# An attention head's pauses filled, its queues reordered, and four weight splits moved to a late head

## The chip, the cores and the metric

The kernel runs on one core of a Trainium2 chip, as one launch. The metric is the device time of that launch in microseconds (us). TensorE (PE) multiplies matrices, its weight loads are listed apart (PEld), VectorE (DVE) and ScalarE (ACT) work on both on-chip memories, GpSimd (POOL) on SBUF alone, and SyncE (SP) issues most of the DMAs. Each engine runs its own queue in order; engines wait for one another by semaphores.

## The reference

Two batches of eight heads of attention, in which a query sees only the keys of its own hash bucket, then a layer of eight experts in which each token goes to its two best, then a second layer in which it goes to one. Only the attention is changed here:

```python
q_bits = (np.einsum('bhsd,dk->bhsk', q, proj) > 0).astype(np.int64)   # 6 bits; the same for k
mask = q_bucket[:, :, :, None] == k_bucket[:, :, None, :]
scores = np.where(mask, scale * np.matmul(q, k.transpose(0, 1, 3, 2)), -1e9)
attn = np.exp(scores - np.max(scores, axis=-1, keepdims=True))
attn = attn / (np.sum(attn, axis=-1, keepdims=True) + 1e-09)
out = np.matmul(attn, v)                       # q, k, v: (2, 8, 768, 64)
```

## The kernel before, in words

**Heads and blocks.** The 16 heads (two batches of eight) run one after another, 768 queries against 768 keys each. The keys are cut into six tiles of 128. The work is software-pipelined: while head i is computed, the maxima of head i+1 are taken, and head i+2 is loaded and prepared. The order of everything is written out by hand: `FIRST` (L1617) for head 0 and `STEPS` (L1609) for the others are six blocks of words, and `step` carries out one word after the other. A word such as `split 0 2 v p` names the step, the head relative to i, the tile, and the engines (a ScalarE, v VectorE, p GpSimd). Instructions stand in each engine's queue in that order.

**The steps of a head.** `hi` and `lo` cut the queries (`QA`, `QB`) and keys (`KA`, `KB`) into a rounded part and a rest (L216 or L218, L223). `hash` (L229) multiplies by the projection, `mask` (L235) turns the signs into rows of QA and KA. `max` (L244, L246) multiplies 128 queries with all keys on TensorE, and VectorE reduces the product to one column; `neg` and `row` (L250, L256, L260) put the six results back into QA as a row. `scores` (L275, L278) are four matmuls of 384 columns and the exponential on ScalarE (L280, tile `P`, two buffers). `split` copies P into a rounded `Ph` (L216 on ScalarE or L218 on VectorE) and subtracts it, `Pl` = P - Ph (L287, on GpSimd; tile 5, and all tiles of the last head, on VectorE). `values` (L298) are six matmuls of 386 columns with Ph and Pl. `z` (L265) is an activation on ScalarE that each head has once, near its end; `mean`, `turn` and `out` finish the head before.

**Buffers.** Every `max`, `scores`, `hash`, `row`, `mean` and `turn` takes one of three PSUM tiles named `big`. A matmul into one waits until the reader of its former content is done. The matmuls without use, `warm(n)` (L193), multiply constants of 512 columns in bf16 into the tile `pv`; before the loop over the heads they stand between the first steps.

**Weight splits.** The experts' weights arrive as halves of 512 KB (tile `wst`, four buffers; four are loaded in head 1). `Experts.split` rounds one half on ScalarE (`whi`, L486), subtracts on VectorE (`wlo`, L489), and asks SP for the next half (the fourth early split asks for none). Four splits are done early, one each in heads 4 to 7 at the word `x` in block 1. The list `early` holds such work with its place, (head, "x") or (head, block); `extra` runs it there.

**Gates of the first batch.** In heads 8 to 15 the list has the routing of the first batch: `parts` (four small VectorE steps, L562 to L565, head 13), `hot` (six comparisons against slot numbers, L644, head 14), `trim` (L616, L617: which of the first 128 places overflow, head 14 behind `hot`), `table` and `fetch` (head 14, block 2), `turn` (head 15).

Of the kernel before, what the change touches and what calls it, by code (L numbers as in the profile page):

```python
# [373 lines left out]
class Experts:  # L374
# [327 lines left out]
    def turn(self, X, xs, u, st, ps=None):  # L702
        nc = self.nc
        xh, xl = X[:, 0], X[:, 1]
        sz = u.sizes[st]
        if ps is None:
            ps = self.mp.tile([128, 4, 128], F32, name="pt", bufs=2)
        for kt in range(4):
            nc.tensor.transpose(ps[:, kt, 0:sz], xs[st][0:sz, kt * 128:(kt + 1) * 128], self.ident[0:sz, 0:sz])
        s = slice(st * 128, st * 128 + sz)  # L710
        nc.scalar.activation(xh[:, :, s], ps[:, :, 0:sz], AF.Copy)
        nc.vector.tensor_sub(xl[:, :, s], ps[:, :, 0:sz], xh[:, :, s].bitcast(F32))  # L712
# [903 lines left out]
)  # L1616
FIRST = (  # L1617
# [6 lines left out]
)  # L1624
# [2 lines left out]
def lsh_moe_kernel(tc, qk, v, proj, w_gate, w_noise, noise, w1, w2, w2_gate, w21, w22, cst_in, out):  # L1627
    nc = tc.nc
    with ExitStack() as ctx:
# [11 lines left out]
        with ExitStack() as actx:  # L1641
            xp = actx.enter_context(tc.tile_pool(name="xp", bufs=3))
            at = Attention(tc, actx, qk, v, cst)
            X = {}
            n = B * H

            def big():
                return at.pb.tile([128, 2, 512], F32, name="big")

            def done(i):  # L1650
                b, h = divmod(i, H)
                if h % 4 == 0:
                    X[b, h // 4] = xp.tile([128, NJ, DM // 2], F32, name="x")
                return at.c_out(i, X[b, h // 4], lg[:, b], i == n - 1)

            def store(b, c0, c1):
                nc.sync.dma_start(xd[b * S:(b + 1) * S, c0:c1].rearrange("(p j) d -> p j d", j=NJ), X[b, c0 // 256][:, :, c0 % 256:(c1 - 1) % 256 + 1])

            def after(i):
                b, h = divmod(i, H)  # L1660
                if h in (3, 5, 7):
                    store(b, *{3: (0, 256), 5: (256, 384), 7: (384, 512)}[h])

            at.load(0)
            at.setup(proj)
            nc.sync.dma_start(cst[:, 128:], cst_in[:, 128:C_CUT])
            nc.sync.dma_start(cst[:, 0:128], cst_in[:, 0:128])
            at.consts2()
            at.load(1)
            nc.sync.dma_start(at.mask, cst_in[96:96 + NJ, C_MASK:C_MASK + S])  # L1670
            at.gate_consts(w_gate, w_noise)
            at.load_v(0)
            at.load_v(1)
            at.load(2)
            at.load_v(2)
            at.warm(9)
            at.a_hash(0)
            at.warm(5)
            at.a_hi(0, "KA")
            at.a_hi(0, "QA", nc.vector)  # L1680
            at.a_mask(0, "KA")
            at.a_mask(0, "QA", slice(0, 1))
            at.a_mask(0, "QA", slice(1, 2))
            at.a_hi(0, "KB")
            at.a_hi(0, "QB")
            at.a_lo(0, "KB", nc.gpsimd)
            at.a_lo(0, "QB", nc.gpsimd)
            for j in range(NJ):
                at.b_max(0, j)
                at.warm((1, 1, 1, 1, 0, 0)[j])  # L1690
                if j == 1:
                    at.a_hi(1, "KA")
                    at.a_hi(1, "QA")
                if j == 4:
                    at.v_hi(0, nc.gpsimd)
                    at.v_lo(0, nc.gpsimd)
            ex = Experts(tc, cst, consts, wpool, ((w1, w2), (w21, w22)), noise, w2_gate, at, lg,
                         ld[:, :], [t[:, :] for t in td])
            ex.carry = carry
            ex.rows_in = cst_in[:, C_ROWS:C_END]  # L1700
            at.b_neg(0)
            at.a_hash(1)
            at.b_row(0, 2)
            at.a_mask(1, "QA")
            at.a_mask(1, "KA")
            at.a_hi(1, "KB")
            at.a_hi(1, "QB")
            early = []

            *_, chain = gates = ex.gate1(0)  # L1710
            scale = gates[0]
            ratio, first, parts = ex.weights1(0)
            hot, table, fetch, turn = ex.early_table(Unit(0, 128, 0, range(0, NJ)), at.wk, big, xd[0:S, :])
            for i in range(4):
                early.append(((4 + i, "x"), lambda i=i: ex.split(i % 2)))
            for (h, s), f in (
                    ((0, 4), scale), *(((1, "x"), f) for f in chain[0:2]), ((2, "x"), chain[2]),
                    *(((3, "x"), f) for f in chain[3:]), ((3, 5), lambda: ex.ranks(slice(0, NJ), big()[:, 0])),
                    ((4, "x"), ratio), ((4, "x"), first), ((5, "x"), parts),
                    ((6, "x"), lambda: hot((0, 1, 2))), ((6, "x"), lambda: hot((3, 4, 5))), ((6, "x"), ex.trim),  # L1720
                    ((6, 2), table), ((6, 2), fetch), ((7, "x"), lambda: ex.rest_ranks(big()[:, 0])),
                    ((7, 2), lambda: turn(0))):
                early.append(((H + h, s), f))

            def extra(i, s):
                for at_, f in early:
                    if at_ == (i, s):
                        f()

            def step(i, s, op):  # L1730
                o, *a = op.split()
                k = i + int(a[0])
                a = a[1:]
                if not 0 <= k < n:
                    return
                e = [dict(a=nc.scalar, v=nc.vector, p=nc.gpsimd)[x] for x in a if x in "avp"]
                if o in ("scores", "values"):
                    getattr(at, "c_" + o)(k, int(a[0]))
                elif o == "split":
                    if k == n - 1:  # L1740
                        e[1] = nc.vector
                    at.c_split(k, int(a[0]), *e)
                elif o in ("move", "mean", "turn"):
                    getattr(at, "c_" + o)(k)
                elif o == "out":
                    done(k)
                    after(k)
                elif o == "x":
                    extra(i, "x")
                elif o == "load":  # L1750
                    at.load(k)
                    at.load_v(k)
                elif o == "max":
                    at.b_max(k, int(a[0]))
                elif o in ("neg", "row"):
                    getattr(at, "b_" + o)(k)
                elif o == "hash":
                    at.a_hash(k)
                elif o == "mask":
                    at.a_mask(k, a[0])  # L1760
                elif o in ("hi", "lo"):
                    getattr(at, "a_" + o)(k, a[0], e[0])
                elif o == "z":
                    at.z_row(k)
                elif k % 2 == 0:
                    getattr(at, o)(k, e[0])

            for i in range(n):
                nx, n2 = i + 1 < n, i + 2 < n
                for s in range(NJ):  # L1770
                    for op in (FIRST if i == 0 else STEPS)[s]:
                        step(i, s, op)
                    extra(i, s)
                    if i == 1 and s == 3:
                        for _ in range(NST):
                            ex.load()
                    if i in (2, 3, 4, 5) and s == 3:
                        ex.clear(yd[:, :], i - 2)
            ps = big()[:, 0]
            u0 = Unit(0, 128, 0, range(0, NJ))  # L1780

            def rows(*r):
                ex.early_rows(u0, *r, ps)

            at.c_values(n - 1, 4)
            rows(0, 4)
            at.c_values(n - 1, 5)
            at.c_move(n - 1)
            rows(4, 9)
            at.c_mean(n - 1)  # L1790
            rows(9, 12)
            at.c_turn(n - 1)
            rest = done(n - 1)
            rest()
            after(n - 1)
# [39 lines left out]
```

## Time and profile before

| | |
|---|---|
| median of 3 runs | 855.6 us (855.22 to 859.2) |
| the profiled execution's own time | 851.21 us |
| its span, first to last instruction | 849.4 us |
| mean granted TensorE clock in it | 0.976 |
| head 0, its scores to its `z` | about 17 to 36 us |
| heads 1 to 15, `z` to `z` | 13.7 to 18.8 us each, the last `z` at 286.5 us |

The page of the profile gives each engine's busy share and a strip of 40 slices; the views used below are the instructions in order of time (the timeline), and the busy time of every engine in chosen stretches (windows). A row of windows has, in this order: the stretch, its length, the busy time and the instructions of PE, PEld, DVE, ACT and POOL, the granted share of TensorE's full clock, the DMA engines' busy share and GB/s. The stretches called heads here run from one `z` (L265) to the next: that of head i holds its blocks 0 to 3, and blocks 4 and 5 of head i-1. The attention ends at about 296 us; the two expert layers take the rest and are not changed.

### The profile page before, as it was taken

How to read it: one execution, taken by the hardware profiler on the slowest of the kernel's cores; microseconds unless marked ns; L12 is line 12 of the kernel's file. 1: busy time of each engine (PE TensorE's matmuls, PEld its weight loads, DVE VectorE, ACT ScalarE, POOL GpSimd, SP SyncE). 2: the span in 40 equal slices, each digit the busy share in tenths (PEclk: the TensorE clock that was granted, in tenths of full speed). 3: DMA queues.
4: the chain of work that ended last, by engine and by line, in shares of the span. 5: the costliest groups of instructions: out<-in, count | busy, mean ns of one | idle time of the engine just before them, and what ended most of it. 6: DMA issues, size and time to landing. Idle time of an engine off the chain costs nothing. (4 is left out here: it accounts for less than half of the span.)

```text
span 849.4 us, 14032 instructions
## 1 busy us (share of the span) xinstructions
PE 798.8 (94%) x5260; PEld 721.9 (85%) x5260; DVE 568.2 (67%) x1086; ACT 466.2 (55%) x649; POOL 378.2 (45%) x302
## 2 busy tenths in 40 slices
PE   7799999999999995899999999999999889999996
PEld 3688777878887784899999999999998789999996
DVE  7688899879897573566645453546485767875654
ACT  5688989898886641244343443334342235555653
POOL 7568776767676015551415050504121253444221
PEclk9899999999999996899999999999999999999999
DMA  5135264022011023266444453435231727787871
GB/s 138 42 116 186 69 222 118 1 75 51 7 38 32 1 69 113 63 203 205 135 167 142 135 194 108 151 124 191 94 129 61 242 83 228 247 262 244 254 247 50
DMA packets 84773, 111.17 MB, mean 131 GB/s; under 512 B 20975, under 2 KB 59007, under 8 KB 84700
## 3 DMA queue, kind: packets, MB, share of 16 engines
q1 hardware_dynamic: 75164, 86.76, 32.5%
q0 software_dynamic: 9312, 23.25, 8.0%
q8 instruction: 44, 0.72, 0.4%
q14 instruction: 29, 0.24, 0.1%
q10 hardware_dynamic: 224, 0.20, 0.1%
HBM read 90.95 MB, written 19.72 MB: 130 GB/s over the span
## 5 line engine op out<-in xcount | busy, mean ns | idle before, releaser
L489 DVE TENSOR_TENSOR wlo<-wst,whi 128x1024 fp32r<-128x1024 f32 x129 | 157.1, 1231 | 36.3 <-ACT whi L486 35.9
L287 POOL TENSOR_TENSOR Pl<-P,Ph 128x768 fp32r<-128x768 f32 x75 | 145.4, 1945 | 73.5 <-ACT Ph L216 30.3
L486 ACT ACTIVATE whi<-wst 128x1024 fp32r<-128x1024 f32 x129 | 134.1, 1053 | 11.5 <-DMA wst<-in_moe_w_dram 11.3
L737 PE MATMUL mm<-xh,whi 128*128 128x400 f32 (+7 forms) x416 | 135.0, 325 | 4.0 <-issue 2.1
L738 PE MATMUL mm<-xh,whi 128*128 128x400 f32 (+7 forms) x416 | 131.9, 317 | 1.8 <-DVE xh L712 1.0
L739 PE MATMUL mm<-xh,wlo 128*128 128x400 f32 (+7 forms) x416 | 131.6, 316 | 1.5 <-issue 1.4
L743 ACT ACTIVATE hh<-mm 128x400 fp32r<-128x400 f32 (+7 forms) x104 | 45.4, 440 | 151.9 <-PE mm L739 123.0
L737 PE MATMUL mm<-hh,whi 128*128 128x400 f32 (+5 forms) x320 | 107.8, 337 | 1.0 <-issue 1.0
L738 PE MATMUL mm<-hh,whi 128*128 128x400 f32 (+5 forms) x320 | 104.7, 327 | 0.3 <-issue 0.3
L739 PE MATMUL mm<-hh,wlo 128*128 128x400 f32 (+5 forms) x320 | 104.4, 326 | 0.0
L280 ACT ACTIVATE P<-big 128x768 f32<-128x768 f32 x96 | 77.6, 809 | 38.1 <-PE big L278 30.0
L744 DVE SCALAR_TENSOR_TENSOR hh<-mm,hh 128x400 fp32r<-128x400 f32 (+7 forms) x104 | 50.6, 490 | 68.9 <-issue 37.1
L246 DVE TENSOR_REDUCE mx<-big 128x1 f32<-128x768 f32 x96 | 88.4, 952 | 11.2 <-PE big L244 9.9
L737 PEld LDWEIGHTS mm<-xh,whi 128*128 128x128 f32 x416 | 79.9, 192 | 5.1 <-issue 2.3
L738 PEld LDWEIGHTS mm<-xh,whi 128*128 128x128 f32 x416 | 80.0, 192 | 3.8 <-issue 2.5
L739 PEld LDWEIGHTS mm<-xh,wlo 128*128 128x128 f32 x416 | 80.1, 193 | 1.7 <-issue 1.7
L828 POOL DMA_INDIRECT ld<-lr,gsi x18 | 21.9, 1219 | 128.9 <-DVE lr L855 127.7
L216 ACT ACTIVATE Ph<-P 128x768 fp32r<-128x768 f32 x80 | 67.7, 846 | 2.0
L738 PEld LDWEIGHTS mm<-hh,whi 128*128 128x128 f32 x320 | 61.2, 191 | 0.5 <-issue 0.5
L739 PEld LDWEIGHTS mm<-hh,wlo 128*128 128x128 f32 x320 | 61.3, 192 | 0.4 <-issue 0.4
L737 PEld LDWEIGHTS mm<-hh,whi 128*128 128x128 f32 x320 | 61.0, 191 | 0.7 <-issue 0.5
L244 PE MATMUL big<-KA,QA 128*128 128x384 f32 x192 | 52.7, 370 | 7.3 <-DVE mx L246 3.6
(329 smaller groups left out, 1707.9 us busy)
## 6 DMA issues: line engine op xcount, KB each, us to landing
wst<-in_moe_w_dram SPq DMA_DIRECT2D x128, 512.0 KB
yd<-zero SPq DMA_DIRECT2D x4, 1536.0 KB
qk<-in_qk_dram SPq DMA_DIRECT2D x15, 384.0 KB
v<-in_v_dram SPq DMA_DIRECT2D x16, 192.0 KB
xd<-x SPq DMA_DIRECT2D x2, 768.0 KB
xd<-x SPq DMA_DIRECT2D x4, 384.0 KB
td<-pay,off POOLq DMA_INDIRECT x36
rio<-in_const_dram SPq DMA_DIRECT2D x1, 384.0 KB
```

The costliest lines, as they stand in the source:

```text
L216: eng.activation(o, x, AF.Copy)
L244: nc.tensor.matmul(ps[:, c, 0:HALF], W["QA"][:, j * 128:(j + 1) * 128], W["KA"][:, c * HALF:(c + 1) * HALF], start=True, stop=True)
L246: nc.vector.tensor_reduce(T["mx"][:, j // 2, j % 2:j % 2 + 1], ps[:, :, 0:HALF], axis=AX.XY, op=OP.max)
L280: nc.scalar.activation(P, ps[:, :, 0:HALF], AF.Exp, scale=1.0 / math.sqrt(D))
L287: second.tensor_sub(Pl, P, Ph.bitcast(F32))
L486: nc.scalar.activation(hi[:, s], st, AF.Copy)
L489: eng.tensor_sub(lo[:, s], st, hi[:, s].bitcast(F32))
L737: nc.tensor.matmul(o, wh, ab[:, 0, k, 0:C], start=(k == 0), stop=False)
L738: nc.tensor.matmul(o, wh, ab[:, 1, k, 0:C], start=False, stop=False)
L739: nc.tensor.matmul(o, wl, ab[:, 0, k, 0:C], start=False, stop=(k == last))
L743: nc.scalar.activation(hh[:, f, 0:C], o, AF.Relu)
L744: nc.vector.scalar_tensor_tensor(hl[:, f, 0:C], o, 0.0, hh[:, f, 0:C].bitcast(F32), op0=OP.max, op1=OP.subtract)
```

## The change

Three edits. In `FIRST`, 13 matmuls without use are put into blocks 0 and 1 (5 behind `scores 0 1`, 4 behind `max 1 0`, 4 behind `max 1 1`), and the subtraction `lo 1 QB` on GpSimd moves from block 3 to block 1, behind `split 0 1`. The four early weight splits move from heads 4, 5, 6, 7 (at `x`) to head 14 (n - 2), to the ends of its blocks 0, 1, 2 and 3, where they stand ahead of `table`. `trim` moves from head 14, behind `hot`, to head 13, behind `parts`.

```diff
 FIRST = (
-    ("scores 0 0", "split 0 0 a p", "scores 0 1", "max 1 0", "hi 2 KB a",),
-    ("max 1 1", "max 1 2", "split 0 1 a p", "max 1 3", "scores 0 2", "hi 2 QB a", "v_hi 2 a",),
+    ("scores 0 0", "split 0 0 a p", "scores 0 1", "warm 5", "max 1 0", "warm 4", "hi 2 KB a",),
+    ("max 1 1", "warm 4", "max 1 2", "split 0 1 a p", "lo 1 QB p", "max 1 3", "scores 0 2", "hi 2 QB a", "v_hi 2 a",),
     ("values 0 0", "hi 2 KA a", "max 1 5", "lo 1 KB v",),
-    ("load 3", "split 0 2 v p", "lo 2 KB v", "scores 0 3", "hi 2 QA a", "max 1 4", "lo 1 QB p", "split 0 3 a p", "neg 1", "values 0 1", "scores 0 4", "v_lo 2 v",),
+    ("load 3", "split 0 2 v p", "lo 2 KB v", "scores 0 3", "hi 2 QA a", "max 1 4", "split 0 3 a p", "neg 1", "values 0 1", "scores 0 4", "v_lo 2 v",),
...
             for i in range(4):
-                early.append(((4 + i, "x"), lambda i=i: ex.split(i % 2)))
+                early.append(((n - 2, i), lambda i=i: ex.split(i % 2)))
...
-                    ((4, "x"), ratio), ((4, "x"), first), ((5, "x"), parts),
-                    ((6, "x"), lambda: hot((0, 1, 2))), ((6, "x"), lambda: hot((3, 4, 5))), ((6, "x"), ex.trim),
+                    ((4, "x"), ratio), ((4, "x"), first), ((5, "x"), parts), ((5, "x"), ex.trim),
+                    ((6, "x"), lambda: hot((0, 1, 2))), ((6, "x"), lambda: hot((3, 4, 5))),
...
                 o, *a = op.split()
+                if o == "warm":
+                    return at.warm(int(a[0]))
```

## Rows read from the trace of the kernel before

**Rows 1.** Page, part 1: engine, busy us (share of span), instructions
```profile
PE 798.8 (94%) x5260; PEld 721.9 (85%) x5260; DVE 568.2 (67%) x1086; ACT 466.2 (55%) x649; POOL 378.2 (45%) x302
```
**Rows 2.** Windows from `z` to `z`, heads 3 to 8 and 14
```profile
69.71:85.39 15.68, 15.68 (x93) 13.70 (x91) 13.12 (x20) 14.01 (x18) 13.58 (x9) 1.00 0.76 252
85.39:102.51 17.12, 16.69 (x93) 13.43 (x91) 15.40 (x18) 15.56 (x19) 11.76 (x8) 1.00 0.15 54
102.51:119.41 16.90, 16.73 (x93) 13.30 (x91) 15.70 (x22) 14.83 (x18) 12.56 (x8) 1.00 0.75 260
119.41:136.52 17.11, 16.64 (x93) 13.43 (x91) 15.37 (x18) 15.57 (x20) 11.68 (x8) 1.00 0.28 105
136.52:153.55 17.03, 16.69 (x93) 13.32 (x91) 15.71 (x22) 14.84 (x19) 12.50 (x8) 1.00 0.36 94
153.55:169.76 16.21, 16.21 (x93) 13.44 (x91) 14.17 (x18) 14.73 (x18) 11.97 (x8) 1.00 0.00 0
254.02:272.79 18.77, 17.07 (x102) 13.95 (x101) 16.69 (x34) 10.74 (x13) 12.56 (x9) 1.00 0.05 15
```
**Rows 3.** Windows of one microsecond in head 0, where the clock falls and rises
```profile
23.00:24.00 1.00, 0.00 (x0) 0.00 (x0) 0.96 (x1) 0.02 (x1) 0.90 (x1) 0.96 0.00 0
24.00:25.00 1.00, 0.96 (x3) 0.97 (x4) 0.00 (x0) 0.00 (x0) 0.77 (x1) 0.50 0.00 0
30.00:31.00 1.00, 1.00 (x5) 1.00 (x5) 0.65 (x1) 0.95 (x2) 0.00 (x0) 0.63 0.00 0
```
**Rows 4.** Timeline, head 0: start, us, engine, line, what, [idle before <-releaser]
```profile
8.60 2.07 PE L193 MATMUL pv<-const-bfloat16-1.0 128*128 128x512 bf16 x5
...
24.04 1.65 PE L244 MATMUL big<-KA,QA 128*128 128x384 f32 x4 [1.05 <-DVE mx L246]
...
32.84 2.45 POOL L287 TENSOR_TENSOR Pl<-P,Ph 128x768 fp32r<-128x768 f32 x1 [8.07 <-DVE Ph L218]
...
35.37 2.44 POOL L223 TENSOR_TENSOR QB<-qk,QB 64x768 fp32r<-64x768 f32 x1
...
37.89 3.33 POOL L287 TENSOR_TENSOR Pl<-P,Ph 128x768 fp32r<-128x768 f32 x2
...
39.62 0.57 PE L298 MATMUL pv<-Pl,vh 128*65 128x386 f32 x2 [1.75 <-POOL Pl L287]
```
**Rows 5.** Timeline, head 4: the two instructions of a split
```profile
92.85 1.06 ACT L486 ACTIVATE whi<-wst 128x1024 fp32r<-128x1024 f32 x1
...
93.94 1.23 DVE L489 TENSOR_TENSOR wlo<-wst,whi 128x1024 fp32r<-128x1024 f32 x1 [0.32 <-ACT whi L486]
```
**Rows 6.** Timeline, head 14: VectorE, GpSimd, TensorE and ScalarE around the splits' new places
```profile
259.88 2.09 POOL L287 TENSOR_TENSOR Pl<-P,Ph 128x768 fp32r<-128x768 f32 x1 [0.28 <-POOL QB L223]
...
260.45 1.82 DVE L246 TENSOR_REDUCE mx<-big 128x1 f32<-128x768 f32 x2
...
261.47 0.96 PE L244 MATMUL big<-KA,QA 128*128 128x384 f32 x4
...
262.19 1.06 DVE L644 TENSOR_SCALAR oh<-slots,r 128x128 bf16<-128x128 f16 x6
...
263.14 1.70 POOL L287 TENSOR_TENSOR Pl<-P,Ph 128x768 fp32r<-128x768 f32 x1 [1.17 <-ACT Ph L216]
263.17 1.71 DVE L616 TENSOR_SCALAR a<-r 128x6 bf16<-128x6 f32 x1
...
...
266.00 0.45 PE L309 MATMUL big<-tr,oT 65*128 65x81 f32 x2 [1.65 <-DVE mx L246]
...
270.12 0.96 DVE L246 TENSOR_REDUCE mx<-big 128x1 f32<-128x768 f32 x1 [0.83 <-PE big L244]
...
276.46 0.81 ACT L280 ACTIVATE P<-big 128x768 f32<-128x768 f32 x1 [0.28 <-POOL Pl L287]
```
**Rows 7.** Timeline, head 13: the end of `parts`, and GpSimd's next subtraction
```profile
246.71 0.19 DVE L565 TENSOR_TENSOR vals<-gm,vals 128x6 bf16<-128x6 f32 x1
...
247.19 1.70 POOL L287 TENSOR_TENSOR Pl<-P,Ph 128x768 fp32r<-128x768 f32 x1 [1.31 <-ACT Ph L216]
```

## The prediction

> **What bounds the kernel now.** First the page's first part: TensorE is busy for 94% of the span [rows 1]. So look where it is not, and ask of every other engine only whether it makes TensorE wait. Then windows from head to head [rows 2]: heads 3 and 8, which carry nothing but attention, have PE busy for their whole length, 15.68 us (an odd head) and 16.21 us (an even one, which also splits v). Heads 4 to 7 carry one weight split each and take 16.90 to 17.12. Head 14 takes 18.77 with PE idle for 1.7 and VectorE busy for 16.69: there VectorE sets the pace. Then head 0 in windows of a microsecond [rows 3] and in order of time [rows 4]: the granted clock falls from 1.00 to 0.50 (2.4 to 1.2 GHz) near 24.0 and is back at about 30.7. Before it fell, PE had stood idle three times for about a microsecond while VectorE reduced a maximum (the wait of 1.05 before the maximum at 24.04 is the last). Later PE waits 1.75 at 39.62 for GpSimd's Pl.
>
> **Edit 1, the 13 matmuls.** Five took 2.07 us at the half clock [rows 4], so about 1.04 at the full one, and four 0.83. The three pauses, about 1.1 each, hold 5, 4 and 4: they fit, and `max` waits for VectorE (or, the first time, for its key rows) as before. Nothing else queues behind them: they write `pv`, which no one holds until `values 0 0`. Without the cover, which means at the half clock, five would end a microsecond late. Their worth is the clock. Four `max` matmuls took 1.65 at the half clock [rows 4] and 0.96 at the full one [rows 6]: 0.17 each. Between the fall and GpSimd's Pl of tile 2 (32.84) the chain is max, scores 2, values 0, max 5 on PE, then VectorE's reduction, a `lo`, and the copy Ph: 14 matmuls, 14 x 0.17 = 2.4, of which I count **-2.2**, since part of the last pause stays. If the clock falls all the same: 0.
>
> **Edit 1, the moved `lo`.** From 32.84 on GpSimd is the chain of head 0: Pl of tile 2 (2.45), `lo 1 QB` (2.44), then Pl of tiles 3 and 4 (3.33), and PE waits for them at 39.62. GpSimd was idle for 8.07 before 32.84 [rows 4]; there the `lo` now runs at no cost. Its 2.44 is 0.74 more than a subtraction alone (1.70 [rows 6]); this was a wait for VectorE's v subtraction beside it, and it falls on Pl of tile 3 instead. So **-1.7**, bounds -1.0 and -2.44. What is late next: Pl of tile 4 then follows its own copy Ph, and ScalarE's exponential of tile 5 follows Pl of tile 3, both about 3.9 earlier than before. SP's `load 3` stands in block 3 as before; it and the first weight loads can only come sooner, into a time when the DMA engines are idle [rows 3]. Head 0 together: **-3.9**. The heads behind it are bound by PE and carry the shift on.
>
> **Edit 2, taken from heads 4 to 7.** Those four took 17.12 + 16.90 + 17.11 + 17.03 = 68.16. Two clean even and two clean odd heads are 2 x 16.21 + 2 x 15.68 = 63.78 [rows 2]: -4.4. With all four as long as the even one it is -3.3. I take **-4.2**, near the first, whose odd head is a row of its own. It is less than the four `wlo` on VectorE (1.23 each [rows 5]), which is plausible: PE bounds these heads once VectorE stops doing so.
>
> **Edit 2, added to head 14.** Head 14 prepares no later head, so ScalarE has room (10.74 busy of 18.77 [rows 2]); VectorE has not. Follow VectorE's queue [rows 6].
> - Before: the two reductions end at about 262.2, `hot` follows, `trim` stands 1.71 beside GpSimd's Pl (263.14 to 264.84), and its reductions let PE go on at 266.00.
> - `wlo` 0 comes behind the first reduction (261.4). GpSimd's Pl runs until 259.88 + 2.09 = 261.97; VectorE's own two-input subtraction waits until then, +0.56, and takes 1.23. The second reduction ends at about 264.05 instead of 262.2, and PE's scores of tile 2 wait for it.
> - `hot` would start at 264.05, but the next Pl (1.70, about 0.1 late because `whi` 0 pushes ScalarE back) lies at 263.2 to 264.9. `trim`, of the same operation as `hot`, waited in just that place; so I let `hot` wait 0.85. With `trim` gone (1.71 and a second step as small as L565's 0.19 [rows 7]) the reduction that PE waits for ends 0.9 later than before.
> - `wlo` 1 and 2 add 1.2 each, since GpSimd is idle then; the 0.83 for which VectorE waited at 270.12 takes some back. `table` stands behind `wlo` 2, so its gather on GpSimd, and Pl of tiles 2 and 3 behind that, come about 3.3 later: 0.9 + 2.4. The exponential of tile 4 needs the buffer of tile 2, so it is 2.9 late.
> - `whi` 3 (1.06 [rows 5]) stands behind that exponential, and the copies of tiles 4 and 5 behind it: 2.9 + 1.06 = 3.9 late. `wlo` 3 stands ahead of the row that scores 15 0 needs; this row had over a microsecond to spare, and comes 4.3 late at scores 15 0.
> - The exponential of head 15's first tile (276.46) waited for Pl of tile 4, and does so again, 3.8 to 3.9 later. From there head 15 goes on as before.
>
> **+3.8**, net of `trim`. Bounds: -1.9 (the splits cost nothing, `trim`'s 1.71 + 0.19 is won) and +9.8 (each of the four waits for a whole Pl: 4 x (1.23 + 1.70) - 1.9). The three weight loads (512 KB each) that follow the splits move along; SP holds them until each `wlo` has freed a buffer, the store of x stands behind them with time in hand, the DMA engines are 5% busy in this head [rows 2], and the halves are needed only after the attention. Whether `hot` waits, no row shows directly. The Trainium skill, "SBUF — State Buffer", section "Who interferes with whom", says that VectorE and GpSimd share a port pair that one holds for its whole instruction, that a VectorE op with two SBUF inputs contends for it with a GpSimd op that reads SBUF, that `tensor_scalar` can too in its two-port modes, and that a reduction never does. `trim`'s 1.71 agrees. By that rule `hot` waits; without it head 14 would cost +2.8, which is the second rival.
>
> **Edit 3, `trim` in head 13.** Two small steps behind L565, which ends at 246.90; GpSimd's next Pl starts at 247.19 [rows 7]. Two times 0.19 lies on this edge. If they get in, +0.3 at most, since PE is the bound there; if the second is caught, up to 1.70 + 0.19 = +1.9. I take **+0.3**.
>
> **Sum.** -3.9 - 4.2 + 3.8 + 0.3 = **-4.0 us**. The profiled execution took 851.21 (its span 849.4 and 1.8 around it), so such an execution would take 847.2. The median of the runs is 855.6, 4.4 above that execution; the shift belongs to both, so I predict **851.6 us**.
>
> **Rivals.**
> - *Forecast*, chance 0.44, own range 849.5 to 853.5.
> - *Head 14 has more room* (0.22): `hot` slips in ahead of Pl, or the order around the gather comes out better. For it: ScalarE and GpSimd are half idle there. Against: VectorE is dense for 13 us. Cost +2.8 or less: 850.6, down to 848.
> - *The clock falls in head 14* (0.16): PE gets pauses of one to two microseconds between short bursts from 262 to 270, as in head 0 before 24. For it: that likeness. Against: the pause of 1.65 at 266.00 left the clock at 1.00 [rows 2]. Price as in head 0, 2.2: 853.8.
> - *The matmuls don't hold the clock in head 0* (0.10): only the moved `lo` counts, so 2.2 is lost: 853.8. For it: pauses are left between the last maximum and scores 2. Against: three of four are filled.
> - *Slower* (0.08): the splits and GpSimd's subtractions block each other in head 14. Each `wlo` waits for a whole Pl, +9.8 as above, the clock falls with it, +2.2, and `trim` is caught, +1.9: -3.9 - 4.2 + 9.8 + 2.2 + 1.9 = +5.8, so 861.4. It decides once heads 13 and 14 lose more than the 8.1 that the other heads win. Against: GpSimd is idle when `wlo` 1 and 2 come.
>
> **Chances.** About 0.5% (4.3 us) is what a measurement of this kernel can tell from no change, and the forecast lies just inside it. Faster by more: half of the forecast and the second case, 0.22 + 0.22, and 0.01 from the others: 0.45. Within: 0.22, both 853.8 cases but a little, and a mild form of the last: 0.46. Slower: 0.09. The range 848.0 to 857.0 leaves out the last rival and the far ends.
>
> **What would show it.** Granted clock 1.00 throughout 24 to 31, with L193 in the three pauses. GpSimd's `lo` (L223) near 25, and Pl of tiles 3 and 4 ending near 37.4. The first `z` near 33.9 instead of 36.2. Heads 4 to 7 at 15.7 to 16.2, no L486 there. In head 14 four L489, the first held until GpSimd's Pl ends, and 22 to 23 us from `z` to `z`. L616 at 0.15 to 0.2 in head 13. I am wrong if head 14 grows by less than 2 or more than 6, or if head 0 gains less than 3.

## The result and the profile after

The changed kernel takes **847.0 us** (median of 4 runs, 844.48 to 848.55) against 855.41 (4 runs, 855.19 to 859.2): a ratio of **0.9889, 95% interval [0.9852, 0.9926]**. The forecast was 851.6 and its range ended at 848.0, so the time lies just below it. Its profiled execution took 846.51 (span 844.7, mean granted clock 0.980), 4.70 less than that of before.

Part 1 of the page of after, beside [rows 1]:

```profile
PE 796.4 (94%) x5273; PEld 721.7 (85%) x5273; DVE 566.5 (67%) x1086; ACT 466.7 (55%) x649; POOL 375.4 (44%) x302
```

It tells little: 13 more matmuls, and nearly the same shares. The stretches tell more. Windows of after, heads 1, 5, 7, 13 and 14, in the columns of [rows 2]:

```profile
31.72:46.83 15.11, 14.93 (x85) 12.44 (x84) 12.48 (x18) 13.80 (x17) 12.61 (x7) 1.00 0.52 174
94.90:110.88 15.98, 15.98 (x93) 13.47 (x91) 14.29 (x20) 14.12 (x18) 12.32 (x8) 1.00 0.92 308
127.08:143.03 15.95, 15.95 (x93) 13.50 (x91) 14.27 (x20) 14.13 (x18) 12.25 (x8) 1.00 0.40 101
227.44:243.83 16.39, 16.36 (x93) 13.36 (x91) 15.37 (x27) 14.11 (x17) 12.59 (x8) 1.00 0.14 49
243.83:265.86 22.03, 19.60 (x107) 15.78 (x106) 19.07 (x34) 14.41 (x17) 12.94 (x10) 0.92 0.29 91
```

Heads 5 and 7, which no longer carry a split, have PE busy for their whole length, as heads 3 and 8 had [rows 2]. Head 14 has grown from 18.77 to 22.03, VectorE is busy for 19.07 of it, and its granted clock is 0.92. Side by side, from the first scores of head 0 (L275) to the last `z`, in us:

| stretch | before | after | difference | forecast |
|---|---|---|---|---|
| first scores to first `z` | 19.03 | 15.50 | -3.53 | -2.2 |
| head 1 | 17.38 | 15.11 | -2.27 | -1.7 |
| heads 4 to 7 | 68.16 | 64.34 | -3.82 | -4.2 |
| head 13 | 16.07 | 16.39 | +0.32 | +0.3 |
| head 14 | 18.77 | 22.03 | +3.26 | +3.8 |
| first scores to last `z` | 269.33 | 263.29 | -6.04 | -4.0 |

Heads that are left out differ by 0.1 at most. Outside of the table the two executions differ by -0.91 ahead of the first scores, where nothing was changed, and by +2.3 behind the last `z`, mostly in the expert layers.

**Head 0.** One-microsecond windows of after, the same stretches as in [rows 3]:

```profile
23.00:24.00 1.00, 1.00 (x7) 0.89 (x6) 0.72 (x2) 0.00 (x0) 0.92 (x2) 1.00 0.00 0
24.00:25.00 1.00, 1.00 (x7) 0.79 (x6) 1.00 (x2) 0.46 (x1) 1.00 (x1) 1.00 0.00 0
30.00:31.00 1.00, 0.63 (x5) 0.45 (x5) 0.97 (x3) 0.38 (x2) 1.00 (x2) 1.00 1.08 291
```

The clock stays at 1.00 (2.4 GHz) in these and in every other microsecond from 16 to 34. The timeline of after, head 0, answers to [rows 4]:

```profile
18.49 1.27 PE L193 MATMUL pv<-const-bfloat16-1.0 128*128 128x512 bf16 x5
...
20.24 1.04 PE L193 MATMUL pv<-const-bfloat16-1.0 128*128 128x512 bf16 x4
21.45 0.61 PE L244 MATMUL big<-KA,QA 128*128 128x384 f32 x2 [0.17 <-DVE mx L246]
21.90 1.05 PE L193 MATMUL pv<-const-bfloat16-1.0 128*128 128x512 bf16 x4
22.60 1.13 PE L244 MATMUL big<-KA,QA 128*128 128x384 f32 x4
...
23.95 1.84 POOL L223 TENSOR_TENSOR QB<-qk,QB 64x768 fp32r<-64x768 f32 x1
28.45 4.76 POOL L287 TENSOR_TENSOR Pl<-P,Ph 128x768 fp32r<-128x768 f32 x2 [2.67 <-DVE Ph L218]
...
35.19 0.96 DVE L287 TENSOR_TENSOR Pl<-P,Ph 128x768 fp32r<-128x768 f32 x1 [0.33 <-issue]
35.38 2.48 POOL L223 TENSOR_TENSOR QB<-qk,QB 64x768 fp32r<-64x768 f32 x1
```

The pauses are filled and the `lo` runs at 23.95, as forecast. Two things were not. The third maximum (the first two of the four matmuls from 22.60) starts while VectorE is still reducing the second, which it does until 23.06; in [rows 4] it waited for that reduction. And Pl of tile 5, on VectorE at 35.19, now starts 0.19 ahead of GpSimd's next `lo` and takes 0.96. Before, it stood behind GpSimd's Pl, and that `lo` had begun at 41.30:

```profile
41.38 2.59 DVE L287 TENSOR_TENSOR Pl<-P,Ph 128x768 fp32r<-128x768 f32 x1 [2.07 <-POOL Pl L287]
```

(the timeline of before, VectorE). There TensorE's next weights and the next exponential then waited 0.3 and 0.2 for it; in after nothing does.

**Heads 13 and 14.** Timeline of after; it answers to [rows 7] and [rows 6]:

```profile
236.32 0.17 DVE L616 TENSOR_SCALAR a<-r 128x6 bf16<-128x6 f32 x1
236.53 0.19 DVE L617 TENSOR_TENSOR a<-a 128x6 bf16<-128x6 bf16 x1
...
249.70 2.10 POOL L287 TENSOR_TENSOR Pl<-P,Ph 128x768 fp32r<-128x768 f32 x1 [0.28 <-POOL QB L223]
251.14 1.73 DVE L489 TENSOR_TENSOR wlo<-wst,whi 128x1024 fp32r<-128x1024 f32 x1
252.96 1.68 POOL L287 TENSOR_TENSOR Pl<-P,Ph 128x768 fp32r<-128x768 f32 x1 [1.16 <-ACT Ph L216]
253.67 1.83 DVE L644 TENSOR_SCALAR oh<-slots,r 128x128 bf16<-128x128 f16 x6
253.80 0.71 PE L275 MATMUL big<-QB,KB 128*128 128x384 f32 x2 [1.55 <-DVE mx L246]
257.15 1.21 DVE L489 TENSOR_TENSOR wlo<-wst,whi 128x1024 fp32r<-128x1024 f32 x1
259.54 1.22 DVE L489 TENSOR_TENSOR wlo<-wst,whi 128x1024 fp32r<-128x1024 f32 x1
261.12 1.19 POOL L691 DMA_INDIRECT xg<-xd,gi  x1 [6.49 <-DVE tg L674]
262.33 3.35 POOL L287 TENSOR_TENSOR Pl<-P,Ph 128x768 fp32r<-128x768 f32 x2
264.08 0.81 ACT L280 ACTIVATE P<-big 128x768 f32<-128x768 f32 x1 [2.64 <-POOL Pl L287]
...
265.87 1.24 DVE L489 TENSOR_TENSOR wlo<-wst,whi 128x1024 fp32r<-128x1024 f32 x1 [1.78 <-ACT whi L486]
```

Read it down VectorE's queue. `wlo` 0 takes 1.73 beside GpSimd's Pl, `wlo` 1 and 2 take 1.2 each with GpSimd idle. `hot` takes 1.83 where it took 1.06 [rows 6], while Pl runs from 252.96 to 254.64: it does wait. The reduction at 252.80, between `wlo` 0 and `hot`, took its usual 0.95. That is what the Trainium skill says in "SBUF — State Buffer", section "Who interferes with whom"; the trace agrees. Counted from the `z` that begins the head, the gather and the two Pl follow 2.9 late and the exponential of tile 4 2.3 late (forecast 3.3 and 2.9), and head 14 grew by 3.26. `trim` costs 0.17 and 0.19 in head 13; its second step starts 0.15 ahead of GpSimd's next Pl (236.68), so it got in on the edge that the forecast names.

The 1.55 for which PE waits at 253.80 brings in the rival that I had priced apart, the fall of the clock. Windows of after:

```profile
254.00:255.00 1.00, 1.00 (x5) 0.91 (x5) 1.00 (x4) 0.00 (x0) 0.64 (x1) 0.59 0.92 271
255.00:256.00 1.00, 1.00 (x5) 0.71 (x4) 1.00 (x5) 0.75 (x2) 0.00 (x0) 0.50 0.75 260
```

The clock does fall there, and is back at 1.00 by 258. VectorE is busy all of that time, so the fall may have cost nothing; e5 below tells.

### The profile page after: what moved, and what is told of

It reads as the page before. It is cut to its first block, busy times and chain, and to the rows that moved or that the text cites. A ratio compares the mean times of both kernels' runs of the same rounds, so it can differ in the third digit from the quotient of the medians.

```text
span 844.7 us, 14064 instructions
## 1 busy us (share of the span) xinstructions
PE 796.4 (94%) x5273; PEld 721.7 (85%) x5273; DVE 566.5 (67%) x1086; ACT 466.7 (55%) x649; POOL 375.4 (44%) x302
## 5 line engine op out<-in xcount | busy, mean ns | idle before, releaser
L828 POOL DMA_INDIRECT td<-pay,off x36 | 38.7, 1074 | 44.4 <-DVE off L596 30.2
```

Source lines behind the costliest of these rows:

```text
L828: ins = self.nc.gpsimd.indirect_dma_start(out=dst, out_offset=off, in_=src, in_offset=None, bounds_check=last, oob_is_err=False)
```

## The experiments

The table above leaves open which edit each gain belongs to, why the third maximum stopped waiting, and whether the -8.4 between the two medians (855.41 and 847.0) is the change or partly the spread between executions. The whole time of one kernel spreads by several microseconds, so the stretches of the table were read as well, from the one profiled execution of each kernel.

**One edit at a time: e1 to e4.** e1 has the 13 matmuls alone, e2 the moved `lo` alone, e3 both, e4 the splits in head 14 with `trim` left there.

```diff
# e1 (e3 too), ... stands for the rest of a line:
+    ... "scores 0 1", "warm 5", "max 1 0", "warm 4", ...
...
+    ... "max 1 1", "warm 4", "max 1 2", ...
# e2 (e3 too):
+    ... "split 0 1 a p", "lo 1 QB p", "max 1 3", ...
...
-    ... "max 1 4", "lo 1 QB p", "split 0 3 a p", ...
+    ... "max 1 4", "split 0 3 a p", ...
# e4:
- early.append(((4 + i, "x"), lambda i=i: ex.split(i % 2)))
+ early.append(((n - 2, i), lambda i=i: ex.split(i % 2)))
```

> Only the 13 matmuls are added to the kernel before. Theory: they hold the clock at 1.00 through 24 to 31 us (2.2 us), and because the planner of PSUM tiles sees other times, the third maximum of head 0 gets another tile and no longer waits for VectorE (1.0 to 1.4 us); the moved subtraction is missing, so GpSimd still holds Pl of tiles 3 and 4 back. The last z comes 3.2 to 3.6 us earlier, measured from the first scores; the time falls by about 3.4, to 852. Rival, the clock alone: 2.2, to 853.2, and the third maximum waits for VectorE as before.

> Only the subtraction lo 1 QB is moved. Theory: worth 1.7 us, as forecast: 853.7; the clock falls near 24 us as before and the third maximum waits. Rival: what head 0 won beyond the forecast (1.9 us) comes from this move, because VectorE's Pl of tile 5 gets in ahead of GpSimd: 3.6 us, 851.8.

> The 13 matmuls and the moved subtraction together, splits and trim as before. Theory: the last z, measured from the first scores, comes 5.8 us earlier, as in the changed kernel's heads 0 and 1; the time falls by 5 to 6.5, to about 849.5. Rival, the forecast's size with chance at the start of the launch and in the expert layers: 3.9, 851.5.

> Only the four splits move to head 14; trim stays in head 14 behind hot. Theory (VectorE's queue sets head 14): heads 4 to 7 win 3.8 us, head 14 grows by 3.3 and by the 1.7 to 1.9 of trim on top, net +1 to +1.5: about 856.6. Rival (ScalarE's copies set head 14, so trim does not matter): head 14 grows by 3.3 only, net -0.5: 854.9.

| kernel | to first `z` | head 1 | heads 4 to 7 | head 14 | all to last `z` | ratio to before [95%] |
|---|---|---|---|---|---|---|
| before | 19.03 | 17.38 | 68.16 | 18.77 | 269.33 | (852.93 us) |
| e1 | 15.46 | 17.39 | 68.18 | 18.77 | 265.82 | 0.9975 [0.9954, 0.9996] |
| e2 | 19.02 | 15.12 | 68.22 | 21.83 | 270.23 | 0.9989 [0.9966, 1.0011] |
| e3 | 15.51 | 15.10 | 68.19 | 18.57 | 263.36 | 0.9946 [0.9924, 0.9967] |
| e4 | 19.03 | 17.42 | 64.32 | 24.59 | 271.33 | 1.0005 [0.9984, 1.0025] |

In these stretches the gains of edit 1 add: the matmuls are worth 3.57, the `lo` 2.26 and that in head 1. (The whole times give less, -2.1 and -0.9 for e1 and e2 and -4.6 for e3, with intervals of about 2 either way.) The splits take 3.84 out of heads 4 to 7 and bring more than that to head 14: e4 ends 2.0 later, where +1 to +1.5 was expected. e2 shows something else: its head 14 has the instructions of before and still takes 21.83. Windows of head 14 and of one microsecond in it, e2:

```profile
250.96:272.79 21.83, 20.17 (x102) 16.68 (x101) 17.10 (x34) 10.75 (x14) 13.14 (x10) 0.84 0.07 21
...
266.00:267.00 1.00, 1.00 (x7) 1.00 (x7) 0.24 (x1) 0.85 (x1) 0.98 (x2) 0.50 0.00 0
```

and PE's only long pause there, timeline of e2:

```profile
262.95 0.45 PE L309 MATMUL big<-tr,oT 65*128 65x81 f32 x2 [1.64 <-DVE mx L246]
```

Before, PE paused for 1.65 at the same instruction [rows 6] and the clock stayed at 1.00 [rows 2]; here it fell to 0.50 two microseconds later. Over the kernels whose head 14 is that of before, it takes 18.6 to 18.8 where the clock stays at 1.00 (before, e1, e3, e10) and 21.5 to 21.8 where it falls (e2, e9). These kernels differ elsewhere, but no edit of theirs lies in head 14, so a single profile's head 14 has to be taken as uncertain by 3 us.

**Where to put the splits: e5 to e8,** one comparison, in which the kernel before took 829.73 (18 runs). e5 is the changed kernel again; e6 is before with `trim` moved and nothing else; e7 is the changed kernel with the splits back in heads 4 to 7, their subtraction on GpSimd; e8 has the four roundings on ScalarE in head 14 and the subtractions on VectorE in blocks where it is not the pace.

```diff
# e6, against before:
- ((5, "x"), parts),
+ ((5, "x"), parts), ((5, "x"), ex.trim),
...
- ((6, "x"), lambda: hot((3, 4, 5))), ((6, "x"), ex.trim),
+ ((6, "x"), lambda: hot((3, 4, 5))),
# e7, against the changed kernel:
- early.append(((n - 2, i), lambda i=i: ex.split(i % 2)))
+ early.append(((4 + i, "x"), lambda i=i: ex.split(i % 2, nc.gpsimd)))
# e8, against the changed kernel (apart[0]: the ACTIVATE of whi, apart[1]: the subtraction and the next load):
- early.append(((n - 2, i), lambda i=i: ex.split(i % 2)))
+ apart = ex.apart(4)
+ for i, at_ in enumerate(((n - 2, 1), (n - 2, 1), (n - 2, 1), (n - 2, 2))):
+     early.append((at_, apart[0][i]))
+ for i, at_ in enumerate(((n - 2, 4), (n - 2, 4), (n - 1, 0), (n - 1, 2))):
+     early.append((at_, apart[1][i]))
```

> The changed kernel again, in more rounds. Theory: the stretches that its trace shows add up to -6.0 us (first scores to first z -3.5, head 1 -2.3, heads 4 to 7 -3.8, head 13 +0.3, head 14 +3.3); the rest of the first comparison, -8.4, was the spread of single executions before the first scores and in the expert layers. Ratio 0.993. Rival: the edits are worth 8.4 and the expert layers gain with them: 0.990.

> Only trim moves to head 13. Theory: in head 14 it stood 1.7 us beside GpSimd's Pl and PE waited for it; in head 13 it gets in ahead of Pl at 0.2 a step. Head 14 falls from 18.8 to between 16.2 and 17, head 13 grows by 0.3: -1.7 to -2.4. Rival: trim is caught by Pl in head 13: head 13 +1.0 or more, net -1 or nothing.

> The changed kernel, but with the four splits back in heads 4 to 7 and their subtraction on GpSimd instead of VectorE. Theory: heads 4 to 7 lost 0.9 each because VectorE's queue was full; GpSimd has 4 to 5 us idle in each, so they come to 16.2 and 16.0, 0.3 more at most; head 14, without splits and trim, to 16.2: in all -11 us against the kernel before, about 4 to 5 under the changed kernel. Rival: GpSimd's subtraction (some 2.3 us) shuts VectorE's two-input subtractions out and delays Pl, so heads 4 to 7 take 17 or more, as before: -7.5.

> The changed kernel, but each split in two: the four copies on ScalarE in blocks 1 and 2 of head 14, where it idles, the four subtractions on VectorE behind the row of head 14 (two) and in blocks 0 and 2 of head 15, where it idles. Theory: VectorE's queue ahead of the row sets head 14, so head 14 falls from 22.0 to 16.5 to 17.2 and head 15 grows by 0.5 at most: about -11 against the kernel before. Rival: ScalarE's copies delay the exponentials by as much as the subtractions did: head 14 at 20, -8.

| kernel | heads 4 to 7 | head 13 | head 14 | head 15 | all to last `z` | ratio to before [95%] |
|---|---|---|---|---|---|---|
| before (profile of the first comparison) | 68.16 | 16.07 | 18.77 | 13.67 | 269.33 | (829.73 us) |
| e5, changed again | 64.34 | 16.39 | 24.20 | 13.68 | 265.41 | 0.9928 [0.9897, 0.9958] |
| e6, `trim` only | 68.21 | 16.38 | 16.93 | 13.67 | 267.88 | 0.9971 [0.9945, 0.9997] |
| e7, GpSimd | 65.89 | 16.38 | 16.94 | 13.68 | 259.82 | 0.987 [0.9832, 0.9908] |
| e8, apart | 64.37 | 16.42 | 17.21 | 14.30 | 259.14 | **0.9854 [0.9823, 0.9885]** |

`trim` moved alone is worth -1.84 in head 14 for +0.31 in head 13. So the four splits alone cost head 14 22.03 - 16.93 = 5.1, or 7.3 in e5, to save 3.8: moved there whole, they lose.

e5 and the execution of after are the same program, and they price the fall of the clock. Windows of e5, its head 14 and two microseconds in it:

```profile
243.24:267.44 24.20, 21.01 (x106) 17.29 (x105) 19.17 (x34) 14.40 (x17) 13.09 (x10) 0.86 0.29 93
254.00:255.00 1.00, 1.00 (x7) 0.68 (x5) 1.00 (x7) 0.74 (x2) 0.04 (x1) 1.00 1.01 360
...
262.00:263.00 1.00, 1.00 (x5) 0.72 (x4) 0.61 (x1) 0.00 (x0) 1.00 (x1) 0.50 1.01 359
```

and its gather in the timeline:

```profile
260.53 1.19 POOL L691 DMA_INDIRECT xg<-xd,gi  x1 [6.49 <-DVE tg L674]
```

In e5 the clock is 1.00 until 259, in after it had fallen at 254. The gather starts 17.29 behind the `z` that begins the head in both (260.53 - 243.24, 261.12 - 243.83). So the fall in after cost nothing: VectorE set the pace there, and the 5.1 is the price of the splits at the full clock. In e5 the clock fell from 259 to 266, and head 14 took 2.17 more.

Windows of e7 (head 4) and of e8 (head 14):

```profile
79.31:95.79 16.48, 16.46 (x93) 13.37 (x91) 14.48 (x16) 15.57 (x20) 13.88 (x9) 1.00 0.17 58
```
```profile
243.85:261.06 17.21, 17.17 (x102) 13.89 (x101) 15.16 (x32) 14.42 (x18) 12.63 (x9) 1.00 0.06 16
```

In both PE is busy all the time at a clock of 1.00. e8 moves the same work to the end of the attention and pays 0.9 (0.28 in head 14, 0.62 in head 15, a little over the 0.5 expected) for 3.8; VectorE gets its part only once head 14's reductions are through. Timeline of e8, the eight instructions of the splits:

```profile
253.93 3.89 ACT L509 ACTIVATE whi<-wst 128x1024 fp32r<-128x1024 f32 x4
...
261.37 2.43 DVE L514 TENSOR_TENSOR wlo<-wst,whi 128x1024 fp32r<-128x1024 f32 x2
268.04 1.22 DVE L514 TENSOR_TENSOR wlo<-wst,whi 128x1024 fp32r<-128x1024 f32 x1
270.89 1.23 DVE L514 TENSOR_TENSOR wlo<-wst,whi 128x1024 fp32r<-128x1024 f32 x1
```

e7 (817.97 us) and e8 (817.86) beat both the kernel before (829.73) and the changed one (823.9), and can't be told from one another.

**Why the third maximum stopped waiting: e9 and e10.** The tiles `big` get their places in PSUM (banks) when the program is built. In the program before, the second and third maxima of head 1 both lie in bank 4; with the 13 matmuls the build places the third in bank 0. Which counts do this was read from built programs: (5, 0, 0) does, (2, 4, 4) doesn't. That parts the clock from the tile.

```diff
# e9, against before, ... stands for the rest of a line:
+    ... "scores 0 1", "warm 2", "max 1 0", "warm 4", ...
...
+    ... "max 1 1", "warm 4", "max 1 2", ...
# e10, against before:
+    ... "scores 0 1", "warm 5", "max 1 0", ...
```

> The kernel before with 2, 4 and 4 matmuls without use in the three places (10 instead of 13). In the built program the third maximum of head 1 keeps the PSUM tile of the second, as before; with 5, 4 and 4 the build gave it another. Theory (the clock is one gain, the tile another): the third maximum waits for VectorE's reduction as before, some 1.0 behind its matmuls without use's cover (it starts 6.9 behind the first scores, as before), the granted clock stays at 1.00 from 16 to 32, and the first scores to the first z take 16.5 to 17.0 us (before 19.03; 2.2 of the clock). Rival (the clock alone is worth all 3.5): 15.5 although the third maximum waits. Second rival (two matmuls in the first pause do not hold the clock): it falls near 24 and the stretch takes 19.0.

> The kernel before with 5 matmuls without use in the first place alone. In the built program the third maximum of head 1 gets the other PSUM tile, as in the changed kernel; the two later pauses stay empty. Theory (two gains): the third maximum starts without a wait for the second's reduction, about 1.2 to 1.4 earlier than the 6.9 behind the first scores of before; if the clock still falls near 24 the first scores to the first z take 17.4 to 18.0 us. Rival (the clock alone is worth all 3.5): with a fall of the clock 19.0, without one 15.5. If the clock stays up here, both say 15.5, and the run tells only that one filled pause is enough.

Timeline, TensorE in head 0, e9 and then e10:

```profile
23.12 0.97 PE L244 MATMUL big<-KA,QA 128*128 128x384 f32 x4 [0.17 <-DVE mx L246]
24.80 0.61 PE L275 MATMUL big<-QB,KB 128*128 128x384 f32 x2 [0.70 <-DVE mx L246]
```
```profile
19.81 0.59 PE L244 MATMUL big<-KA,QA 128*128 128x384 f32 x2
21.45 0.98 PE L244 MATMUL big<-KA,QA 128*128 128x384 f32 x4 [1.05 <-DVE mx L246]
23.12 0.62 PE L244 MATMUL big<-KA,QA 128*128 128x384 f32 x2 [0.69 <-DVE mx L246]
23.57 0.51 PE L275 MATMUL big<-QB,KB 128*128 128x384 f32 x2
```

e9: the clock is 1.00 in every microsecond from 16 to 32, the third maximum waits until 23.12, and scores 2 wait 0.70 more for a reduction and start at 24.80. First scores to first `z`: **16.80**, so the clock alone is worth 2.23, and not all 3.5 (15.5), nor nothing (19.0). e10: the third maximum follows the second at once (the four matmuls from 21.45), scores 2 start without a wait at 23.57, the clock stays at 1.00 too, and the stretch is **15.46**, as with all 13. The tile is worth 16.80 - 15.46 = **1.34**. That e10's clock stayed up is what I had not expected: five matmuls in the first pause were enough in the execution profiled, and both gains come with them. The whole times (e9 0.9996 [0.9967, 1.0025], e10 0.9979 [0.9947, 1.0012], before 854.28) can't show 2 or 3 us; e9's profile fell into a long head 14, 21.50 at a clock of 0.84.

## Why the prediction was wrong

The time lies 4.6 under the forecast. Of this 2.0 are in the attention, and the step of the prediction that failed there is that the third maximum waits as before; the `lo` and the splits were mis-sized besides. The other 2.6 lie in the base from which the 4.0 were subtracted, and stay open.

- **Edit 1, the matmuls: -2.2 forecast.** The step, 14 matmuls at 0.17 each less a remainder, was right: -2.23 in e9. What failed is the sentence that "`max` waits for VectorE ... as before". The added matmuls changed which place in PSUM the third maximum got, and with it waits went: -1.34 more (e9 against e1 and e10).
- **Edit 1, the `lo`: -1.7 forecast, -2.27 measured** (-2.26 alone in e2). I had followed GpSimd's queue and not Pl of tile 5 on VectorE, behind it. Once the `lo` was gone this Pl started before GpSimd's next `lo` and took 0.96 instead of 2.59. That this is where the other 0.6 came from is read from the traces, and no run shows it apart.
- **Heads 4 to 7: -4.2 forecast, -3.82 measured.** The odd heads among them take 15.95 to 15.98 and not head 3's 15.68.
- **`trim`: +0.3 forecast, +0.32 measured.** Its -1.9 in head 14 is -1.84 in e6.
- **Head 14: +3.8 forecast, +3.26 and +5.43 measured** (after, e5). The steps of VectorE's queue came in the order told, `hot`'s wait too; from the gather on they are 0.4 to 0.6 less late than the sum has it. But the rival "the clock falls in head 14" (0.16) was true as well: in after, e4 and e5, each time. In after the fall cost nothing; in e5 it came later, from 259 to 266, and cost 2.17, the 2.2 of that rival. That +3.26 lies so near +3.8 is in part luck in where the clock fell.
- **The other rivals.** "Head 14 has more room" fell with `hot`'s wait, though +3.26 is halfway to it. "The matmuls don't hold the clock" fell with the windows, and "slower" with head 14 far from +9.8.
- **Sum and base.** The attention gained 6.04 in the profile where I had 4.0, 2.0 of it by the terms above. The remaining 2.6 between 851.6 and 847.0 is not in the attention. I set the shift against 855.6, the median of three runs; against the profiled execution, 851.21, it gave 847.2, and that of after took 846.51. In the comparison of e1 to e4 35 runs of the same kernel spread from 848.4 to 856.3 with a median of 852.9, in that of e9 and e10 13 runs from 849.1 to 856.5 with 854.3; 852.9 - 6.0 = 846.9. In the comparison of e5, with more runs, the change measured 0.9928, 5.8 us, and not 8.4. So the rest fits the spread of the kernel before, which is arithmetic and not shown. The -0.91 ahead of the first scores looks like chance as well: e1, e2 and e4 start their scores at 16.2, e3 at 16.9.

In the profiled executions edit 1 makes the gain. e3, which is edit 1 alone, has 263.36 to the last `z`, and the whole change 263.29 and 265.41: moving the splits, with `trim`, brought nothing or lost 2 us. In e3 the clock stayed up in head 14, and how often it does is not known for either kernel; the whole times (0.9946 [0.9924, 0.9967] for e3, 0.9889 [0.9852, 0.9926] and 0.9928 [0.9897, 0.9958] for the change) don't settle it.

## What to carry to other kernels

A matmul added for the clock can change the placement of PSUM tiles and so the waits behind it: compare the placement of the two builds before pricing an instruction at its own duration. Work moved off a lean stretch onto the stretch that its engine paces cost more here than it saved; part it by engine and put each part where that engine idles (e8 paid 0.9 for the splits where the change paid 5.1, and 7.3 with the later fall of the clock). Price a move against more than three runs of the kernel before, and a stretch against more than one profile where the clock can fall in it.

## What the runs showed of the hardware

The clock's fall after like pauses is not settled by the program: the same program let it fall at 254 in after and only at 259 in e5, and after a pause of 1.64 to 1.65 at the same instruction in head 14 it stayed at 1.00 in before and fell to 0.50 in e2. In head 0 it fell after three pauses of about a microsecond [rows 3], in before and e2, and did not in e10, where two were left (1.05 and 0.69).

The kernel before took 852.9 to 855.4 us in three of the comparisons and 829.7 in that of e5 to e8, which ran on another chip. Most of these 23 to 26 us lie in one place. Windows of e10 and of e5 (the other chip), the start of the expert layers:

```profile
310.00:330.00 20.00, 9.82 (x75) 9.27 (x74) 5.06 (x36) 2.05 (x4) 12.62 (x13) 0.64 0.43 120
330.00:350.00 20.00, 16.56 (x199) 15.63 (x198) 11.61 (x62) 2.30 (x6) 9.86 (x10) 0.84 0.16 43
```
```profile
310.00:330.00 20.00, 20.00 (x273) 19.86 (x272) 16.68 (x96) 4.93 (x12) 15.26 (x16) 1.00 0.39 128
330.00:350.00 20.00, 20.00 (x146) 19.75 (x146) 15.35 (x27) 11.65 (x18) 15.88 (x14) 1.00 0.76 246
```

PE is busy for 9.82 and 16.56 at clocks of 0.64 and 0.84, which makes about 9.82 x 0.64 + 16.56 x 0.84 = 20 us of work at the full clock in e10 (an estimate, since the clock is a mean of each stretch), and 40 in e5. Eight small matmuls (L897) in the timelines of after and of e5, one of their groups in after and all eight in e5:

```profile
324.57 0.61 PE L897 MATMUL po<-ig,yt 128*128 128x8 f32 x3 [1.73 <-issue]
```
```profile
314.03 0.95 PE L897 MATMUL po<-ig,yt 128*128 128x8 f32 x8
```

In after PE issues a matmul or two every 0.7 to 2.1 us there, from 313 to 325, waiting for nothing that the profile shows, and the clock falls with it; in e5 the eight take 0.95 together. It is in the kernel before and in the changed one alike (before, 310 to 330: 13.09 busy, 0.86). What causes it was not tried.
